# A cross-covariance attention and feed-forward kernel: the sixteen second products of the first token group placed at steps 11 to 31 instead of 11 to 33

## The chip, the cores and the metric

The kernel runs on one core of a Trainium2 chip. The metric is device time in microseconds (us). Beside it each run gives the span, from the first to the last instruction of the core; the time is some 1.7 to 3.0 us longer than the span. All runs here were classed as fast by the clock and the 1.5% limit, with a granted TensorE clock of 0.999 to 1.000. Engines are called by the profile's names: PE (matmuls), PEld (weight loads), ACT (ScalarE), DVE (VectorE), POOL (GpSimd), SP.

## The reference, cut to what matters

```python
def _attn_ref(q, k, v, tau):               # q, k, v: 4 x 6080 x 256
    qn = q / (np.linalg.norm(q, axis=1, keepdims=True) + 1e-06)
    kn = k / (np.linalg.norm(k, axis=1, keepdims=True) + 1e-06)
    s = kn.transpose(0, 2, 1) @ qn / tau
    a = softmax(s)                          # cut: written out in full
    return v @ a
def _moe_ref(x, w_in, w_out, s, b):         # x: 24320 x 256, d_ff = 2048
    r = np.maximum(x @ w_in, 0.0)
    return (s * (r * r) + b) @ w_out
```

## The kernel before

The attention matrix is folded into the weights of the first product: per batch, `wa` is the softmax times `w_in`. The 24,320 tokens are then taken in 48 groups (47 of 512 and a last one of 256), and each group in 16 steps. A step makes one h tile of 128 of the 2,048 features (two 512-column matmuls); after every second step ACT takes the pair of h tiles out of PSUM as `r = relu(h)`. DVE or ACT squares r to `g`. The second product g x w_out comes later, interleaved with the next group's steps. Groups 1 to 46 use seven instead of eight block products ("seven items" per step), which need sums S of g made on DVE. Groups 0 and 47 are "plain": sixteen second products, one per 128 features, each of four 256-column matmuls (two in group 47).

```python
# pools: h_ps 2 buffers (pairs of h tiles), sq_pool 2, o_ps 3
PLAG = {0: 11, NG - 1: 5}
CO = (7, 14, 18, 24)                  # steps of the four casts of w_out; cast 0 on DVE, 1 to 3 on ACT
RC = (13, 16, 19, 21, 23)             # sums for rowconst on DVE; its matmul is at step 30
# ... cut ...
def norm_step(gr=gr, c=c, sc=sc):     # squares and folds of the next batch's q and k, chunk c
    ops = gr.norm_ops(c)              # ACT square, DVE square, DVE fold, DVE fold, ...
    for i, f in enumerate(ops):
        at_step(int(sc) + 2 + 1 + i * 3, f)
# ... cut ...
for s in range(NS + FT):              # FT = 16 steps per group
    g, m = divmod(s, FT)
    if g < NG:
        mm1(g, m)                     # h of this step
    # ... cut: seven items of the group before ...
    for gp in plain:
        for mp in range(FT):
            if s == gp * FT + PLAG[gp] + (mp * 3 // 2 if gp == 0 else mp):
                plain_mm2(gp, mp)     # after the last one: two o_sb evacuations on DVE
    if g < NG and m % 2 == 1:
        relu(g, m // 2)               # ACT
    # ... cut: squares, sums S, then the side work (casts, norms, gram products) of step s ...
```

The kernel holds each engine's instructions to program order (`tc.keep_in_program_order`), and the traces follow it: putting two evacuations back in the program moved them from 64.79 to 67.70 us on DVE (e1 below). So the position of a product in this loop sets what stands behind it.

Of the kernel before, what the change touches and what calls it, by code (L numbers as in the profile page):

```python
# [16 lines left out]
def kernel(  # L17
# [28 lines left out]
    FT = Dff // P  # L46
# [541 lines left out]
    def mm1(g, m):  # L588

        _, nj = group(g)  # L590
        n = nj * P
        vT = vT_tiles[g]
        i, fh = divmod(m, 2)
        if fh == 0:
            h_tiles[g, i] = h_tile("h_ps")
        h_ps = h_tiles[g, i][:, fh, :]
        for b, p0, p1 in segments(g):
            wa = grams[b].wa
            for ci in range(CH):
                if p1 - p0 == P:  # L600
                    dst, src = h_ps[:, :n], vT[:, ci, :n]
                else:
                    dst = h_ps[:, :n].rearrange("f (j p) -> f j p", p=P)[:, :, p0:p1]
                    src = vT[:, ci, :n].rearrange("f (j p) -> f j p", p=P)[:, :, p0:p1]
                po(nc.tensor.matmul(dst, wa[:, ci, ts(m, P)], src,  # L605
                                    start=(ci == 0), stop=(ci == CH - 1), skip_group_check=True))
        if m == FT - 1:
            del vT_tiles[g]

    def relu(g, i):  # L610
        n = group(g)[1] * P
        if i % 2 == 0:
            r_tiles[g, i // 2] = rpool.tile([P, 2, 2, TG], FP16, tag="r16", name="r16")
        r16 = r_tiles[g, i // 2]
        po(nc.scalar.activation(out=r16[:, :, i % 2, :n], in_=h_tiles.pop((g, i))[:, :, :n],  # L615
                                func=AF.Relu))

    def square(g, i0, i1, engine):

        n = group(g)[1] * P  # L620
        if i0 == 0:
            g_tiles[g] = gpool.tile([P, 2, NP, TG], FP16, tag="g16", name="g16")
        src = r_tiles[g, i0 // 2][:, :, i0 % 2 : i0 % 2 + i1 - i0, :n]
        dst = g_tiles[g][:, :, i0:i1, :n]
        if engine is nc.scalar:
            po(nc.scalar.activation(out=dst, in_=src, func=AF.Square))  # L626
        else:
            po(nc.vector.tensor_mul(dst, src, src))  # L628
# [33 lines left out]
    def plain_mm2(g, m):  # L662

        _, nj = group(g)
        if g == NG - 1:
            last_mm2(0, m)
            if m == FT - 1:
                for i in range(FT):
                    last_mm2(1, i)
            return  # L670
        for h in range((nj + 1) // 2):
            js = [j for j in (2 * h, 2 * h + 1) if j < nj]
            if m == 0:
                o_plain[g, h] = ps_o.tile([P, 2, C], FP32, tag="o_ps", name="o_ps")
            o = o_plain[g, h]
            for j in js:
                po(nc.tensor.matmul(  # L677
                    o[:, j % 2, :], g_tiles[g][:, m % 2, m // 2, ts(j, P)],
                    w_out16[:, m, :], start=(m == 0 and j == js[0]),
                    stop=(m == FT - 1 and j == js[-1]), skip_group_check=True))  # L680
            if m == FT - 1:
                if h == 0:
                    o_sbs[g] = opool.tile([P, TG // P, C], FP32, tag="o_sb", name="o_sb")
                evacuate(o_sbs[g][:, js[0] : js[-1] + 1, :], o, rowconst, 1)
                if js[-1] == nj - 1:
                    store(g)
# [4 lines left out]
    def sums_of(g, n, i0=0, i1=NP):  # L691
        G = g_tiles[g][:, :, i0:i1]
        A11, A12 = G[:, 0, :, : TG // 2], G[:, 1, :, : TG // 2]
        A21, A22 = G[:, 0, :, TG // 2 :], G[:, 1, :, TG // 2 :]
        if i0 == 0:
            S[n] = spool.tile([P, NP, TG // 2], FP16, tag=f"S{n}", name=f"S{n}")
        T = {k: t[:, i0:i1] for k, t in S.items()}
        if n == 1:
            po(nc.vector.tensor_add(T[1], A21, A22))  # L699
        elif n == 2:  # L700
            po(nc.vector.tensor_sub(T[2], T[1], A11))  # L701
        elif n == 3:
            po(nc.vector.tensor_sub(T[3], A11, A21))  # L703
        else:
            po(nc.vector.tensor_sub(T[4], A12, T[2]))  # L705
# [77 lines left out]
    PLAG = {0: 11, NG - 1: 5}  # L783
# [13 lines left out]
    for s in range(NS + FT):  # L797
        g, m = divmod(s, FT)
        if g < NG:
            mm1(g, m)  # L800

        if m == SHIFT and 0 < g and g - 1 not in plain:
            items = seven_items(g - 1)
            work.append((items, 8 if g == NG - 1 else 7))
        if work:
            items, n = work[0]
            for f in items[:n]:
                f()
            del items[:n]
            if not items:  # L810
                work.pop(0)
        for gp in plain:
            for mp in range(FT):
                if s == gp * FT + PLAG[gp] + (mp * 3 // 2 if gp == 0 else mp):
                    plain_mm2(gp, mp)
        if g < NG and m % 2 == 1:
            relu(g, m // 2)
            if g in plain:
                late = g > 0 and m // 2 % 2 == 0
                square(g, m // 2, m // 2 + 1, nc.scalar if late else nc.vector)  # L820
        if g < NG and g not in plain and m in SQUARES:
            square(g, *SQUARES[m])
        if g == NG - 1 and m in LAST:
            LAST[m]()
        elif m == 0 and 0 < g and g - 1 not in plain:
            square(g - 1, 6, 8, nc.vector)
        elif 0 < g and g - 1 not in plain and m in SUMS:
            sums_of(g - 1, SUMS[m])
        for f in side.pop(s, []):
            f()  # L830
# [34 lines left out]
```

## Time and profile before

| | before |
|---|---|
| time, median of 3 (lowest to highest) | 720.33 us (720.29 to 720.56) |
| span of the profiled run | 718.5 us |
| busy PE / DVE / ACT / POOL | 97% / 87% / 76% / 15% |
| PE waits listed after the start-up | 0.4, 0.3 and 0.2 us |

Busy shares are averages over the whole span. PE is busy 49.99 or 50.00 us in every 50 from 100 to 700, so what can be won lies in the stretches where PE is not first. The chain that ended last shows these. Line L605 is h, L677 a plain second product, L773 a block product, L615 relu, L504 a cast of w_out, L633 an evacuation of o_ps (to `o_sb` or `u`), L699 to L705 the sums S, L162, L165 and L178 the norm operations. For PE a record's length runs past the start of the next matmul (57.13 + 0.59 against 57.56), so holes are counted from start to start. The lines themselves stand in the prediction.

### The profile page before, as it was taken

The numbers are of one execution on the slowest core, as the hardware profiler recorded it, in microseconds if no ns is written. First come the engines' busy times: TensorE is split into PE (matmuls) and PEld (weight loads), VectorE is DVE, ScalarE is ACT, GpSimd is POOL, SyncE is SP. The second block draws the span as 40 slices with busy tenths as digits, with TensorE's granted clock in tenths as the row PEclk, the third lists the DMA queues.
The fourth block names the chain that finished last, engine by engine and source line by source line (L and its number), as shares of the span: only waits on it lengthen the run. The fifth ranks groups of instructions, "written<-read, shape, count | busy, mean of one in ns | idle before, by whom it ended". The sixth has DMA issues, their size and how long they took to land.

```text
span 718.5 us, 17642 instructions
## 1 busy us (share of the span) xinstructions
PE 699.4 (97%) x7481; PEld 505.0 (70%) x7481; DVE 625.9 (87%) x879; ACT 544.5 (76%) x588; POOL 109.8 (15%) x189
## 2 busy tenths in 40 slices
PE   4799999999999999999999999999999999999998
PEld 3556777776677777777677777777668777777777
DVE  4779999998889999999888899999887888888886
ACT  4489877887777777788777777778877777777875
POOL 4532332201201222111110222110000000000000
PEclk9999999999999999999999999999999999999999
DMA  9999999547565979443973777844423333321202
GB/s 237 207 259 148 172 166 149 110 103 134 103 105 120 153 133 144 105 96 75 152 155 63 139 136 125 154 93 83 105 65 75 92 71 74 97 59 46 83 30 75
DMA packets 89791, 84.27 MB, mean 117 GB/s; under 512 B 59664, under 2 KB 64848, under 8 KB 89712
## 3 DMA queue, kind: packets, MB, share of 16 engines
q0 software_dynamic: 26064, 43.40, 37.7%
q1 hardware_dynamic: 63072, 38.43, 21.5%
q8 instruction: 59, 0.97, 0.5%
q10 hardware_dynamic: 576, 1.31, 0.5%
q14 instruction: 20, 0.16, 0.1%
HBM read 78.91 MB, written 24.90 MB: 144 GB/s over the span
## 4 chain that ended last, share of the span: by engine, by line
PE 92%; DMA 4%; ACT 1%; DVE 1%; POOL 0%; issue 0%; ACTq 0%; POOLq 0%
PE h_ps L605 45%; PE o_ps L773 40%; PE s_ps L142 4%; PE wa_ps L309 2%; DMA qk<-in_q_dram 2%; DMA qk<-in_k_dram 1%; DMA w_in<-in_moe_w_in_dram 1%; ACT r L615 1%; PE o_ps L651 0%; POOL qk L126 0%; PE o_ps L677 0%; ACT g L626 0%; PE idle_ps L442 0%; DVE o_sb L633 0%; DVE sq L162 0%
## 5 line engine op out<-in xcount | busy, mean ns | idle before, releaser
L615 ACT ACTIVATE r<-h_ps 128x1024 f16<-128x1024 f32 (+1 forms) x384 | 387.6, 1013 | 146.9 <-PE h_ps L605 145.0
L605 PE MATMUL h_ps<-vT,wa 128*128 128x512 f16 (+7 forms) x1632 | 451.9, 364 | 0.6 <-ACT r L615 0.4
L773 PEld LDWEIGHTS <-S 128*128 128x128 f16 x2944 | 197.9, 98 | 85.1 <-DVE S L699 0.4
L773 PEld LDWEIGHTS <-g 128*128 128x128 f16 x2208 | 155.0, 98 | 74.1
L628 DVE TENSOR_TENSOR g<-r 128x2048 f16<-128x2048 f16 (+2 forms) x150 | 174.7, 1165 | 15.1 <-ACT r L615 14.9
L773 PE MATMUL o_ps<-T,S 128*128 128x128 f16 x2208 | 183.2, 219 | 0.3 <-DVE S L699 0.2
L605 PEld LDWEIGHTS <-wa 128*128 128x128 f16 x1632 | 136.0, 98 | 21.4 <-issue 1.0
L773 PE MATMUL o_ps<-w_out,g 128*128 128x128 f16 x1472 | 134.2, 219 | 0.3 <-DVE u L633 0.3
L633 DVE SCALAR_TENSOR_TENSOR o_sb<-o_ps,s_out,u 128x256 f32<-128x256 f32 x138 | 66.4, 481 | 47.6 <-PE o_ps L773 45.1
L626 ACT ACTIVATE g<-r 128x1024 f16<-128x1024 f16 (+1 forms) x97 | 100.4, 1035 | 0.2
L142 PE MATMUL s_ps<-qk 128*128 128x256 f16 (+1 forms) x384 | 70.0, 283 | 14.0 <-ACT qk L133 8.7
L361 POOL DMA_DIRECT2D v<-in_v_dram x48 | 31.3, 656 | 263.0 <-DMA vT<-v 199.5
L633 DVE SCALAR_TENSOR_TENSOR u<-o_ps,s_out,rowconst 128x256 f32<-128x256 f32 x138 | 65.9, 478 | 0.0
L773 PE MATMUL o_ps<-w_out,S 128*128 128x128 f16 x736 | 63.4, 219 | 0.0
L773 PE MATMUL o_ps<-N,g 128*128 128x128 f16 x736 | 63.4, 219 | 0.0
L188 POOL DMA_DIRECT2D f<-f x30 | 26.3, 877 | 225.8 <-DVE f L178 167.0
L165 ACT ACTIVATE sq<-qk 128x1024 f16<-128x1024 f16 (+3 forms) x49 | 50.4, 1033 | 10.3 <-DMA qk<-in_k_dram 6.3
L701 DVE TENSOR_TENSOR S<-S,g 128x2048 f16<-128x2048 f16 (+1 forms) x47 | 56.4, 1201 | 1.3
L699 DVE TENSOR_TENSOR S<-g 128x2048 f16<-128x2048 f16 (+1 forms) x47 | 56.0, 1192 | 0.0
L705 DVE TENSOR_TENSOR S<-g,S 128x2048 f16<-128x2048 f16 x46 | 55.9, 1216 | 0.0
L703 DVE TENSOR_TENSOR S<-g 128x2048 f16<-128x2048 f16 x46 | 55.9, 1215 | 0.0
L142 PEld LDWEIGHTS <-qk 128*128 128x128 f16 (+1 forms) x384 | 32.9, 101 | 19.8 <-DVE qk L132 8.1
(75 smaller groups left out, 324.3 us busy)
## 6 DMA issues: line engine op xcount, KB each, us to landing
out_dram<-o_sb SPq DMA_DIRECT2D x46, 512.0 KB, 3.0
v<-in_v_dram POOLq DMA_DIRECT2D x47, 256.0 KB, 4.7
qk<-in_k_dram POOLq DMA_DIRECT2D x42, 256.0 KB, 6.0
qk<-in_q_dram POOLq DMA_DIRECT2D x42, 256.0 KB, 7.2
f<-f POOLq DMA_DIRECT2D x30, 128.0 KB, 3.0
vT<-v SPq DMA_TRANSPOSE x182, 3.2
w<-in_moe_w_out_dram POOLq DMA_DIRECT2D x4, 512.0 KB, 11.4
raw<-in_q_dram ACTq DMA_DIRECT2D x2, 512.0 KB, 6.6
```

Of the source, the lines that this page charges most:

```text
L142: po(nc.tensor.matmul(self.s_ps[:, ch, :], kc[:np_, j, ts(ch, P)], qc[:np_, j, :], start=(c == 0 and j == 0 and ch == 0), stop=(c == len(s ...
L165: po(nc.scalar.activation(out=st["sq"][:np_, 1, js, :], in_=kc[:np_, js, :], func=AF.Square))
L605: po(nc.tensor.matmul(dst, wa[:, ci, ts(m, P)], src, start=(ci == 0), stop=(ci == CH - 1), skip_group_check=True))
L615: po(nc.scalar.activation(out=r16[:, :, i % 2, :n], in_=h_tiles.pop((g, i))[:, :, :n], func=AF.Relu))
L626: po(nc.scalar.activation(out=dst, in_=src, func=AF.Square))
L628: po(nc.vector.tensor_mul(dst, src, src))
L633: po(nc.vector.scalar_tensor_tensor(out=dst, in0=src, scalar=s_out, op0=ALU.mult, in1=add, op1=ALU.add))
L699: po(nc.vector.tensor_add(T[1], A21, A22))
L701: po(nc.vector.tensor_sub(T[2], T[1], A11))
L703: po(nc.vector.tensor_sub(T[3], A11, A21))
L705: po(nc.vector.tensor_sub(T[4], A12, T[2]))
L773: po(nc.tensor.matmul(st[name][:, j, :], a()[:, i, ts(j, P)], w[:, i, :], start=first, stop=last, skip_group_check=True))
```

## The change

It spreads the sixteen plain products of group 0 over steps 11 to 31 instead of 11 to 33. The intent is to place each product, and with it each need for a cast of w_out, where the activations leave PE idle.

```diff
-                if s == gp * FT + PLAG[gp] + (mp * 3 // 2 if gp == 0 else mp):
+                if s == gp * FT + PLAG[gp] + (mp * 4 // 3 if gp == 0 else mp):
```

## The prediction

> **What bounds the kernel now.** I read the page first: its engine shares, its slices, then the chain that ended last. All times are microseconds (us) from the span's start unless another unit is given.
>
> ```profile
> PE 699.4 (97%) x7481; PEld 505.0 (70%) x7481; DVE 625.9 (87%) x879; ACT 544.5 (76%) x588; POOL 109.8 (15%) x189
> PE   4799999999999999999999999999999999999998
> PE 92%; DMA 4%; ACT 1%; DVE 1%; POOL 0%; issue 0%; ACTq 0%; POOLq 0%
> ```
>
> TensorE (PE) ends the kernel: 92% of the chain is its own work. Only 1% is ScalarE (ACT) and 1% VectorE (DVE); that is where a reordering that removes no work could gain anything. The next question is where those stretches lie. The chain in order of time, limited to 49 to 80, answers (start, length, engine and line):
>
> ```profile
> 49.57 1.02 ACT r L615
> 50.59 0.30 ACT w_out L504
> ...
> 55.22 0.94 ACT g L626
> 56.17 0.91 ACT r L615
> 57.08 0.94 ACT g L626
> 58.02 0.92 ACT r L615
> 58.95 0.04 issue
> 58.99 0.59 PE h_ps L605 x2
> ...
> 67.49 1.32 DVE o_sb L633 x2
> 68.82 1.14 DVE S L699
> 69.98 1.23 DVE S L701
> ...
> 74.27 0.41 DVE u L633
> 74.68 0.04 issue
> 74.72 0.22 PE o_ps L773
> ```
>
> The set-up of groups 0 and 1 has two places where PE is not first: from 49.6 to 59.0 ACT carries the chain (activations, casts of w_out, squares), and from 64.6 to 74.7 mostly DVE (evacuation of the first group's output, then the sums S of the second). After 74.7 it is PE again. The PE timeline shows what both cost:
>
> ```profile
> 57.13 0.59 PE L605 MATMUL h_ps<-vT,wa 128*128 128x512 f16 x2
> 57.56 0.60 PE L677 MATMUL o_ps<-w_out,g 128*128 128x256 f16 x4
> 58.00 0.59 PE L605 MATMUL h_ps<-vT,wa 128*128 128x512 f16 x2
> 58.99 0.59 PE L605 MATMUL h_ps<-vT,wa 128*128 128x512 f16 x2 [0.40 <-ACT r L615]
> 70.00 0.45 PE L773 MATMUL o_ps<-T,S 128*128 128x128 f16 x5 [0.20 <-DVE S L699]
> 74.72 0.22 PE L773 MATMUL o_ps<-w_out,g 128*128 128x128 f16 x1 [0.33 <-DVE u L633]
> ```
>
> An "h" pair of matmuls occupies 0.43 between starts (57.13 to 57.56), a "second product" of four small ones 0.44 (57.56 to 58.00). The modelled ends overlap the next start, so I count starts. The h pair at 58.00 should be followed at 58.43; it is followed at 58.99, so the true hole is 0.56, not the listed 0.40. In the same way: 0.09 before 52.50 and 0.29 before 57.13. First-stretch holes: 0.09 + 0.29 + 0.56 = 0.94. In the second: 0.37 before 70.00 (previous two matmuls began at 69.53 and needed about 0.10), a smaller one inside the products near 72.2, and 0.33 before 74.72: some 0.9 together. That 1.8 of 718.5 is all there is to win here.
>
> **What the Trainium skill says.** "TensorE: Matmul & The Clock Gate", section "Wait — 56ns, not 53.3ns?", gives 215.7 ns between starts of warm 512-column matmuls; the trace agrees (0.43 for two). So a PE that is fed has no slack. "ScalarE: Activation LUTs", section "What ACT_TABLE_LOAD costs", has activations with immediate operands at 186 + 0.833 N ns and about 93 ns of overlap between neighbours; for N = 1024 that is 1.04 each, 0.95 start to start. The trace shows 1.02 to 1.08 and 0.91 to 0.94, so ten ACT operations back to back need about 9.3, whatever PE does. "Perfetto Trace Analysis", section "Identifying the Most-Contended Engine", warns that matmul busy share misjudges the distance to a roofline; the trace agrees, since slices marked 9 hide the 0.29 hole before 57.13.
>
> **The change part by part.** Nothing is added or removed: the comparison of instruction orders has equal row counts on every engine. The sixteen second products of group 0 move from steps 11,12,14,15,17,18,20,21,23,24,26,27,29,30,32,33 to 11,12,13,15,16,17,19,20,21,23,24,25,27,28,29,31. ACT keeps its order of operations; on DVE the two o_sb evacuations step ahead of one square (g) and one sq. So the gain is PE work put into holes. I replay the order with the before trace's spacings (h pair 0.43, product 0.44, gram pair 0.22, ACT about 0.93 start to start, 0.05 from ACT end to PE start, 0.03 from PE end to ACT).
>
> 1. *The first cast.* Product 4 now stands at step 16, before h of step 17. It starts at 51.53 by PE's own pace, and the cast of its weights ends at 50.49 + 1.04 = 51.53, plus 0.05: a wait of 0.05.
> 2. *ACT slips.* The h pair of step 17 starts at 52.02 where it started at 51.53, and so its activation at about 52.65 instead of 52.33. From there ACT is saturated through step 26: the whole ACT chain is 0.32 late.
> 3. *PE is fuller.* h of step 26 waits for the activation of step 23, at 58.99 + 0.32 = 59.31. But PE by then has done 12 products instead of 10: 2 x 0.44 = 0.87 more work. Net lead 0.87 - 0.32 = 0.55. The holes on the way become 0.05 (first cast), 0.23 (step 24), 0.13 (step 26), later 0.09 (step 28): 0.50 in place of 0.94, a gain of 0.44 to 0.47. The other casts end 0.2 to 0.9 before they are needed.
> 4. *End of group 0.* The last product starts at 64.38 (was 66.15), h of step 35 at 66.76 (was 67.23): lead 0.47.
> 5. *DVE.* Before, it idled 1.00 ahead of the square at 65.67 (waiting for activation r), then did square, sq and both evacuations in a saturated chain. Now the evacuations (1.32) start at about 64.79, inside that idle time; the square starts at 66.11, sq at 67.25, S (L699) at 67.86 instead of 68.73: 0.87 earlier. Its result is ready at 69.11, and PE wants it at 69.63 - 0.47 = 69.16: the hole of 0.37 closes. The following DVE work (S, u, S, f, sq, u) is saturated and moves by the same 0.87; the second u, which released PE at 74.72, releases it at 73.85.
>
> Sum: 0.47 from PE filling its ACT holes plus about 0.4 from DVE's earlier start, not twice 0.87. PE leaves the second stretch 0.87 earlier. From 75 to 700 PE is busy to 0.05 in every 50, on its own chain, so nothing after should swallow the lead: 720.33 - 0.87 = 719.46, rounded to 719.5.
>
> **Rivals.** *A wait in place of the removed one:* the denser order needs the first and third casts sooner. For it: the first cast has no margin in my replay (51.53 against 51.53), and each 0.1 of wait there also delays ACT's saturated chain. If the wait were 0.4, ACT would be 0.7 late and PE would gain only 0.1 by step 26; the time would be about 719.9 to 720.2. Against it: ACT's order is unchanged and the cast's start hangs on the h pair of step 13, which does not move (48.94).
>
> *ACT stays the bound and takes everything:* it must do the same operations. For it: ten back to back from 49.6 on. Against it: in the old order ACT waited for PE after step 29 (idle 0.49, 0.42, 0.42, 0.20), so a fuller PE recovers there. If all of the ACT slip stuck and DVE gained nothing, the lead would be 0.2: 720.1.
>
> *Hidden or given back:* the DVE gain could be lost if an early operation waits for a transfer rather than for DVE's turn. For it: sq and f wait for loaded qk. Against it: those loads start below 50, and no PE wait for DMA is listed after the start. Then only PE's 0.47 stays: 719.9. Or a later wait for a fixed event returns the time: near 720.3.
>
> **Range and chances.** My replay gives 719.46; partial loss gives 719.9; complete loss 720.3. The three runs before spread 0.27. A gain beyond 1.3 would need nearly all of both stretches' holes to go. I take 719.0 to 720.2. A change of 2% is 14.4, eight times all the holes, so within 2% is practically certain: chances 0.005, 0.99 and 0.005.
>
> **What would show it right or wrong.** Step 1: first product after the cast (L677) at 51.5 to 51.7. Step 2: the casts of w_out at 50.5, 53.6 and 59.1. Step 3: holes in PE starts up to step 29 of about 0.5 in all. Step 4: first L773 product at 67.2 rather than 67.67. Step 5: first o_sb evacuation at about 64.8, S of L699 at 67.9, no PE wait for it, and the u wait ending near 73.9. Span near 717.6. The prediction is wrong if PE waits for the cast by over 0.3, if DVE's S has not moved by more than 0.5, or if a lead at 75 has gone by 700.

## The result, and the profile after

| | before | after |
|---|---|---|
| time, median of 6 | 720.35 us (720.24 to 720.56) | 719.70 us (719.40 to 720.23) |
| span of the profiled run | 718.5 us | 717.6 us |
| spans of the runs after | | 717.5 to 717.9 us |

The ratio is 0.9991, with a 95% interval of 0.9978 to 1.0004. A ratio is computed as the mean time of one kernel's runs over that of the other's of the same rounds, so it is not quite the ratio of the two medians. The interval includes 1: the times alone do not prove a gain. The traces do better: the one kernel that was traced twice (after, and again as e12) took the same PE path to 0.01 us.

The chain of waits after, in order of time, limited to 49 to 80 (start, length, engine and line):

```profile
52.61 1.02 ACT r L615
53.63 0.32 ACT w_out L504
...
56.43 0.92 ACT r L615
57.35 0.04 issue
57.40 0.59 PE h_ps L605 x2
...
64.53 0.23 PE o_ps L677 x2
64.76 0.04 issue
64.79 1.41 DVE o_sb L633 x2
66.20 1.13 DVE g L628
67.33 0.60 DVE sq L162
67.93 1.15 DVE S L699
69.08 0.02 issue
69.11 1.23 DVE S L701
...
73.80 0.04 issue
73.84 0.22 PE o_ps L773
```

ACT carries the chain only up to 57.35 now (before: 58.95). DVE's part starts with the evacuations at 64.79, where before they stood at 67.49 behind the square of group 1. It ends, and PE takes over, at 73.84 instead of 74.72. The timeline of PE after:

```profile
51.54 0.60 PE L677 MATMUL o_ps<-w_out,g 128*128 128x256 f16 x4
57.40 0.59 PE L605 MATMUL h_ps<-vT,wa 128*128 128x512 f16 x2
59.26 0.59 PE L605 MATMUL h_ps<-vT,wa 128*128 128x512 f16 x2
67.18 0.55 PE L773 MATMUL o_ps<-w_out,g 128*128 128x128 f16 x7
69.16 0.44 PE L773 MATMUL o_ps<-T,S 128*128 128x128 f16 x5
73.84 0.22 PE L773 MATMUL o_ps<-w_out,g 128*128 128x128 f16 x1 [0.21 <-DVE u L633]
```

The first S product, at 69.16, follows without a hole (70.00 before). Two later holes stay, counted start to start: 0.25 before 71.55 and 0.49 before 73.84. From 73.84 on PE keeps its lead: the last run of 21 matmuls starts at 711.97, and at 712.80 before. The lead is 0.88 at 73.84 and 0.83 at the end; 0.04 of each was there before the first changed instruction (transposes at 48.45 and 48.49).

### The profile page after: what moved, and what is told of

It is laid out like the page before. It is cut to its first block, busy times and chain, and to the rows that moved or that the text cites. A ratio compares the mean times of both kernels' runs of the same rounds, so it can differ in the third digit from the quotient of the medians. Undisturbed runs are those within 1.5% of the kernel's fastest.

```text
span 717.6 us, 17642 instructions
## 1 busy us (share of the span) xinstructions
PE 699.5 (97%) x7481; PEld 505.1 (70%) x7481; DVE 626.0 (87%) x879; ACT 544.4 (76%) x588; POOL 110.1 (15%) x189
## 4 chain that ended last, share of the span: by engine, by line
PE 93%; DMA 4%; DVE 1%; ACT 1%; POOL 0%; issue 0%; ACTq 0%; POOLq 0%
PE h_ps L605 45%; PE o_ps L773 40%; PE s_ps L142 4%; PE wa_ps L309 2%; DMA qk<-in_q_dram 2%; DMA qk<-in_k_dram 1%; DMA w_in<-in_moe_w_in_dram 1%; PE o_ps L677 1%; PE o_ps L651 0%; ACT r L615 0%; POOL qk L126 0%; PE idle_ps L442 0%; DVE o_sb L633 0%; DVE S L701 0%; DVE sq L162 0%
## 5 line engine op out<-in xcount | busy, mean ns | idle before, releaser
L773 PEld LDWEIGHTS <-S 128*128 128x128 f16 x2944 | 198.0, 98 | 84.8 <-issue 0.4
L773 PEld LDWEIGHTS <-g 128*128 128x128 f16 x2208 | 155.1, 98 | 74.1
L773 PE MATMUL o_ps<-T,S 128*128 128x128 f16 x2208 | 183.3, 219 | 0.1
L773 PE MATMUL o_ps<-w_out,g 128*128 128x128 f16 x1472 | 134.2, 219 | 0.2 <-DVE u L633 0.2
L773 PE MATMUL o_ps<-w_out,S 128*128 128x128 f16 x736 | 63.4, 219 | 0.0
L773 PE MATMUL o_ps<-N,g 128*128 128x128 f16 x736 | 63.4, 219 | 0.0
L699 DVE TENSOR_TENSOR S<-g 128x2048 f16<-128x2048 f16 (+1 forms) x47 | 56.1, 1193 | 0.0
```

The lines of the kernel that those rows point to most:

```text
L699: po(nc.vector.tensor_add(T[1], A21, A22))
L773: po(nc.tensor.matmul(st[name][:, j, :], a()[:, i, ts(j, P)], w[:, i, :], start=first, stop=last, skip_group_check=True))
```

## The experiments

**Theory:** two chains meet in the second stretch. PE must get there, and DVE must get through evacuation, square, S, and two u. PE leaves when the later of the two is done. The change moves both: PE by filling its holes behind ACT, DVE because the evacuations now stand before the square, in idle time. **Main rival:** the gain is PE's filled holes alone, each worth its own length. **Second rival:** the gain is DVE's alone.

To compare runs whose starts differ by up to 0.4 us, I take times from one point ahead of the change, T, the start of the transposes of group 1. P is the first block product (L773), Y the first product of the fourth block product, where PE waited for the second u; E is the start of the last run of matmuls. These are from the PE timelines; V, the start of group 0's evacuations, is from the DVE timelines.

| kernel | T | P | V | Y | E | E - T | against before | median span |
|---|---|---|---|---|---|---|---|---|
| before | 48.49 | 67.67 | 67.41 | 74.72 | 712.80 | 664.31 | | 718.5 to 718.6 |
| after | 48.45 | 67.18 | 64.79 | 73.84 | 711.97 | 663.52 | -0.79 | 717.8 |
| e1 evacuation held | 48.79 | 67.52 | 67.70 | 75.01 | 713.08 | 664.29 | -0.02 | 718.6 |
| e2 last two early | 48.52 | 67.70 | 65.30 | 74.35 | 712.49 | 663.97 | -0.34 | 718.4 |
| e3 front only | 48.55 | 67.28 | 67.37 | 74.67 | 712.75 | 664.20 | -0.11 | 718.4 |
| e4 casts early | 48.50 | 66.73 | 64.60 | 73.65 | 711.74 | 663.24 | -1.07 | 717.4 |
| e6 after, norms later | 48.82 | 67.55 | 65.16 | 73.47 | 711.92 | 663.10 | -1.21 | 717.2 |
| e9 before, norms later | 48.63 | 67.81 | 66.96 | 73.74 | 712.19 | 663.56 | -0.75 | 717.9 |
| e7 cast late | 48.56 | 68.58 | 66.19 | 75.24 | 713.43 | 664.87 | +0.56 | 719.1 |
| e5 casts early, norms later | 48.47 | 66.70 | 64.57 | 72.63 | 711.08 | 662.61 | -1.70 | 716.8 |

Median spans are of 5 runs (after and e13: 6; before: 9 or 10). The runs of e1 to e4 shared one chip and one set of runs before; e5, e6, e7 and e9 shared another of each; e10 to e12 shared a third set of runs before, and e13 had that set and one run more. Outputs were correct in all.

The table holds a regularity that sharpens the theory. In the seven kernels with the norms in their old place (before, after, e1 to e4, e7) Y comes 9.05 after V where the evacuations stand ahead of the square, and 7.30 or 7.31 after V where they stand behind it. So DVE's chain sets Y in all seven, and PE's filled holes count there only as far as they let the evacuations start earlier. Ahead of the square these start 0.42 or 0.43 after the start of the last plain product (after, e2, e7), unless rowconst holds them (e4).

### e1: the change with the evacuations put back behind the square

```diff
-                evacuate(o_sbs[g][:, js[0] : js[-1] + 1, :], o, rowconst, 1)
+                held.append(...)      # the same call, run at step 33
```

> The changed kernel with PE's order kept, but group 0's two o_sb evacuations put back behind the square g and sq on VectorE, as in the kernel before. Theory (the vector chain from evacuation to the sums S to the second u sets when PE leaves the stretch; a PE lead alone is only waited away): first L773 product still at 67.2 us, S of L699 at about 68.7 (not 67.9), a PE hole of about 0.8 us before the first S product at 70.0, u wait ending at 74.7; span 718.4 +- 0.2, no gain over the kernel before. Rival (filling PE's holes is worth its own 0.47 us whatever VectorE does): span 718.0.

PE's order is that of the change. P - T is 18.73, exactly as after (18.73; before 19.18). But DVE is back in its old order, and its timeline and PE's read:

```profile
67.70 1.40 DVE L633 SCALAR_TENSOR_TENSOR o_sb<-o_ps,s_out,rowconst 128x512 f32<-128x512 f32 x2
69.02 1.21 DVE L699 TENSOR_TENSOR S<-g 128x2048 f16<-128x2048 f16 x1
70.29 0.45 PE L773 MATMUL o_ps<-T,S 128*128 128x128 f16 x5 [0.64 <-DVE S L699]
```

PE's lead of 0.45 is waited away in one hole (0.80 start to start, 0.37 before), and E - T is that of the kernel before to 0.02. Main rival refuted: it wanted 0.47. The span of the profiled run, 720.0, missed the expected 718.4, while the other four were 718.3 to 718.6. The excess lies after the work: the last DVE evacuation started at 715.58 (before: 715.30), yet the span ended at 720.0 (before: 718.5); what follows that evacuation is the last store. The ratio of times is 0.9999 (0.9987 to 1.0012).

### e2: the kernel before with only the last two products moved, to steps 30 and 31

```diff
-  (mp * 3 // 2 if gp == 0 else mp)
+  (mp * 3 // 2 - 2 * (mp >= 14) if gp == 0 else mp)
```

> The kernel before with only the last two second products of group 0 moved, from steps 32 and 33 to 30 and 31. PE's holes behind the activations stay (0.94 us in all up to step 29), so PE has no lead at step 35 (first L773 product at 67.6 to 67.7). Theory (vector chain): the evacuations enter VectorE's idle time at about 65.3, S of L699 starts at 68.3 to 68.4, the hole before 70.0 closes, and PE leaves at about 74.35: a gain of 0.35 to 0.45, span 718.1. Rival (only the filling of the holes behind the activations counts): span 718.5.

```profile
65.30 1.41 DVE L633 SCALAR_TENSOR_TENSOR o_sb<-o_ps,s_out,rowconst 128x512 f32<-128x512 f32 x2 [0.17 <-PE o_ps L677]
```

P - T is 19.18, as before: PE gained nothing. The evacuations started at 65.30, as soon as PE's last plain product released them, and S at 68.36, and Y came 0.40 earlier from T than before. E - T fell by 0.34. DVE's half of the change alone gives somewhat less than half of the gain. The profiled span was 718.1, the expected value; the median of five 718.4 and the ratio 0.9994 (0.9982 to 1.0007) cannot tell it from before.

### e3: the change without its last two products

```diff
-  (mp * 4 // 3 if gp == 0 else mp)
+  ((mp * 3 // 2 if mp >= 14 else mp * 4 // 3) if gp == 0 else mp)
```

> The changed kernel with only its last two second products put back to steps 32 and 33; the other fourteen as in the change. Theory (vector chain): PE reaches step 35 with a lead of about 0.45 us (first L773 product at 67.2), but the evacuations start at about 67.4 and S of L699 at 68.7 as in the kernel before; the lead is waited away before the first S product; span 718.4 +- 0.2. Rival (PE's filled holes are worth 0.47 by themselves): span 718.0.

P - T is 18.73: fourteen products suffice for PE's whole lead. S of L699 started at 68.69, and E - T gained 0.11, within what was expected for the span (718.4). With e1 this is the second way to give PE its lead and DVE nothing, and it again yields next to nothing. The halves measured alone, 0.11 and 0.34, add up to 0.45, while both together gave 0.79: they cannot be added. DVE's half keeps its gain alone; PE's half needs it, and on top of it brings 0.45 (0.79 less 0.34).

### e7: the change with cast 1 one step later

```diff
-    CO = (7, 14, 18, 24)
+    CO = (7, 15, 18, 24)
```

> The changed kernel with the cast 1 of w_out at step 15 (behind the activation of steps 14 and 15) instead of step 14. Theory (the product at step 16 has no margin for that cast): the cast runs at about 51.75 to 52.8, product 4 starts at 52.85 instead of 51.54, a PE hole of 1.3 us, and the activations behind it slip by up to as much; some 0.9 to 1.3 us lost against the changed kernel by the first L773 product (68.1 to 68.5), span 718.5 to 719.0, so at or above the kernel before. Rival (ScalarE's total of work is what matters, not the place of a cast): span stays 717.6.

```profile
51.17 0.59 PE L605 MATMUL h_ps<-vT,wa 128*128 128x512 f16 x2
52.94 0.60 PE L677 MATMUL o_ps<-w_out,g 128*128 128x256 f16 x4 [1.18 <-ACT w_out L504]
```

The product should have followed the h pair at 51.60; it started at 52.94, a hole of 1.34. P, V and Y are each 1.29 later from T than after, E - T is 1.35 longer, and the median span of 719.1 is above that of the kernel before. P (68.58) and the span lie just above the expected ranges. The change has indeed no margin at its first cast, and a hole here passes through whole: DVE's evacuations are as late as PE.

### e4: the change with casts 1 and 2 two steps earlier

```diff
-    CO = (7, 14, 18, 24)
+    CO = (7, 12, 16, 24)
```

> The changed kernel with the casts 1 and 2 of w_out moved from steps 14 and 18 to 12 and 16, where ScalarE waits for PE (1.20 and 0.19 us idle), so that they leave its saturated stretch. Both theories: the PE holes before the h pairs of steps 24 and 26 (0.22 and 0.13 us) close, first L773 product at about 66.75 instead of 67.18. Theory (vector chain): the evacuations cannot start before rowconst is done on VectorE (64.65), so S moves by at most 0.2 us; span 717.4. Rival (PE's lead counts in full): span 717.15.

The casts now run where ACT waited for PE. P comes 18.23 after T, 0.50 earlier than after; the holes up to step 26 are gone. But rowconst holds DVE until 64.5, the evacuations started at 64.60 instead of 64.79, and E - T gained only 0.28 over after. So the theory's cap is seen again, near its predicted 0.2. The ratio to before is 0.9975 (0.9962 to 0.9989), the first that excludes 1. It flatters the kernel a little: the nine runs before in this set had a median of 720.89, and 720.35 beside the changed kernel.

### e6 and e9: norm operations of the next batch put off, in the kernel after and the one before

```diff
-                    at_step(int(sc) + 2 + 1 + i * 3, f)
+                    at_step(int(sc) + 2 + 1 + i * 3 + (max(0, 12 - c) if gr.b == 1 else 0), f)
```

> The changed kernel with the norm operations (squares and folds on ScalarE and VectorE) of the second batch's first chunks put off by 12 steps for chunk 0, 11 for chunk 1 and so on, so that none stands on VectorE between the evacuation of group 0 and the second u. Theory (this vector chain holds PE at 71.55 and 73.84): S of L699 starts at 67.25 instead of 67.85, the PE holes of about 0.25 and 0.5 us close, the first Y product starts at about 73.1; span 716.9, if the put-off work costs nothing later. Rival (those holes are PE's own pace or activations): no move, span 717.6.

> The kernel before with the same put-off of the norm operations. Theory (PE's lead of 0.47 and VectorE's lead of 0.87 are not a sum: PE leaves at the later of the two): with VectorE out of the way the evacuations start at 66.8, S at 68.15, all three later PE holes (0.37, 0.25, 0.5) close, span about 717.4; and the difference to the changed kernel with the same put-off shrinks from 0.9 to PE's own 0.45 to 0.55 us. Rival (the gain of the change comes from VectorE alone): with norms put off both kernels have the same span to 0.15.

With squares and folds out of DVE's chain, PE has no hole left between P and Y in either kernel. In e6 the end reads so (six such matmuls take 0.33 from start to start):

```profile
73.14 0.50 PE L773 MATMUL o_ps<-T,S 128*128 128x128 f16 x6
73.47 0.22 PE L773 MATMUL o_ps<-w_out,g 128*128 128x128 f16 x1
```

S of L699 came 0.49 earlier from T than after, where 0.60 was expected. In the kernel before Y falls 1.12 earlier from T, in the kernel after 0.74 earlier. E - T differs between the two by 0.46, and P - T by 0.45: PE's filled holes count in full exactly where DVE no longer sets the end. The second rival, which wanted equal spans, is refuted (medians 717.9 and 717.2).

Both kernels gave 0.32 to 0.37 back: E - Y is 638.07 to 638.19 in all kernels of the table with the norms in their old place, and 638.45 in e5, e6 and e9. Comparing the starts of the same activations after and in e6, the lead shrinks near 100 and near 135 us. So the expected spans were missed, for e6 by 0.3 (median 717.2 for 716.9) and for e9 by 0.5 (717.9 for 717.4).

### e5: casts early and norms later together

The edits are those of e4 and e6, both in the changed kernel.

> The changed kernel with both the casts 1 and 2 at steps 12 and 16 and the norm operations put off. Theory: with VectorE out of the way PE's extra lead of 0.45 from the earlier casts counts in full, where it counted 0.2 to 0.25 with the norms in their old place; the first Y product starts at about 72.65; span 716.4. Rival (rowconst on VectorE caps the start of the evacuations at 64.6 and so everything after): span 716.7, 0.2 below the put-off alone.

Y fell at 72.63 as expected, and the extra PE lead of the early casts counted 0.49 (662.61 against 663.10 in e6), where with the norms in place it had counted 0.28. The span, 716.7 to 716.9 in four of five runs and 718.4 in one, missed 716.4 by the 0.37 that the put-off gives back; the expectation had left that out. It lies near the rival's 716.7, but not for the rival's reason: that wanted a gain of 0.2 over e6, and it was 0.49 in E - T. The ratio to before is 0.9977 (0.9964 to 0.9989). By its trace this is the fastest kernel, 1.70 ahead of before; by times it cannot be told from e4.

### e10, e11, e12, e13: shorter put-offs, and why they fail

```diff
-  (max(0, 12 - c) if gr.b == 1 else 0)          # e5
+  (max(0, 8 - 3 * c) if gr.b == 1 else 0)       # e10
+  (max(0, 12 - 4 * c) if gr.b == 1 else 0)      # e11; e12 is the changed kernel once more
```

> Casts 1 and 2 early, and the norm operations put off by 8 steps for chunk 0, 5 for chunk 1, 2 for chunk 2 and none after. Theory (the put-off of all chunks by up to 12 steps gave back 0.37 us because squares and folds then met later sums on VectorE near 100 and 135 us): the holes of the second stretch stay closed (first Y product near 72.65), the lead is no longer given back, span 716.3 to 716.5. Rival (VectorE must do this work before 150 anyway, and whatever leaves the stretch returns as a hole): span 716.7 to 716.8 as with the long put-off.

> The same with 12, 8, 4 steps and none after. Theory: as the short put-off, span 716.3 to 716.5. Rival: 716.7 to 716.8.

> The changed kernel again, in the same rounds as its two descendants: span 717.5 to 717.9, first L773 product 18.73 us after the first transpose of group 1 (19.18 in the kernel before). Theory and rival agree; it is the yardstick for the other two.

e10, e11 and e13 keep the early casts of e5. Theory and rival were both wrong for e10 and e11: median spans 718.3 and 719.7, E - T 664.10 and 665.64, so up to 3 us worse than e5. The yardstick e12 repeated the changed kernel to 0.01 in E - T (712.26 - 48.74 = 663.52; median span 717.7, ratio 0.9989, 0.9976 to 1.0001). I had moved each chunk by a different amount and so pushed the first four chunks closer together. In e11 the waits read so, first PE's and then ACT's:

```profile
77.35 0.22 PE L773 MATMUL o_ps<-T,S 128*128 128x128 f16 x1 [0.63 <-ACT T L508]
81.99 0.59 PE L605 MATMUL h_ps<-vT,wa 128*128 128x512 f16 x2 [0.48 <-ACT r L615]
85.99 0.45 PE L773 MATMUL o_ps<-T,S 128*128 128x128 f16 x5 [0.61 <-DVE S L699]
89.39 0.33 PE L773 MATMUL o_ps<-T,S 128*128 128x128 f16 x3 [1.03 <-DVE u L633]
79.97 1.06 ACT L165 ACTIVATE sq<-qk 128x1024 f16<-128x1024 f16 x1 [1.75 <-issue]
83.88 1.06 ACT L165 ACTIVATE sq<-qk 128x1024 f16<-128x1024 f16 x1 [1.03 <-issue]
```

The two stalls of ACT name no releaser, but each ends 0.08 after a fold on DVE ends (79.89 and 83.80), and there are two buffers of squares. Test e13 gives e11 four (of the first folds too, which come from the same pool):

```diff
-    sq_pool = pool("sq_pool", 2)
+    sq_pool = pool("sq_pool", 4)
```

> The 12, 8, 4 put-off with the pool of squares at 4 buffers instead of 2. The medium put-off had cost 3.0 us against the long one; its ScalarE trace has two stalls, 1.75 us before the square at 79.97 and 1.03 before that at 83.88, each ending 0.08 us after a fold on VectorE (79.89, 83.80), with activations queued behind. Theory (the two buffers of squares are held by unfinished folds, and ScalarE, in order, makes PE wait): both stalls go, and with them the PE holes at 81.99 (0.54) and, as they come from late activations, most of that at 85.99 (0.61); those at 77.35 (cast of T behind a square, 0.63) and 89.39 (second u behind squares and folds, 1.0) stay; span about 718.6. Rival (crowding of VectorE and ScalarE alone): span 719.5 to 719.8.

```profile
PE o_ps L773 <- DVE u L633: 1.0, 1, 1.0
PE o_ps L773 <- ACT T L508: 0.6, 1, 0.6
```

In the list of PE's waits (waiter, line, releaser: total, times, longest) after the start-up only these two are left of the four. The squares start at 78.09 and 81.87 without a stall, and the profiled span is 718.6 as expected (median 718.8, e11 719.7). From T to E, e11 took 665.64 and e13 664.45 (712.92 - 48.47): the two-buffer pool cost 1.2 of the 3.0 that e11 lost against e5. The rest stands in the waits for a cast of T and for u; that the order of squares and folds made those late is read from the trace, not tested. For e10 the cause was read from its trace alone, in part: it too waits for a cast of T and for u. What e5 gives back near 100 and 135 us was not tested further.

## Why the prediction was right

It said 719.5 with 719.0 to 720.2; the median is 719.70.

- **Step 1, the first cast:** the product was to start between 51.5 and 51.7; it started at 51.54. The lack of margin is shown by e7.
- **Step 2, ACT's slip of 0.32:** casts were to start at 50.5, 53.6 and 59.1; they started at 50.45, 53.53 and 59.08.
- **Step 3, remaining PE holes of 0.50:** counted start to start they are 0.04, 0.22, 0.13 and 0.13, in all 0.52.
- **Step 4, P at 67.2:** 67.18.
- **Step 5, evacuation at 64.8, S at 67.9, no wait for S, u's wait ending at 73.9:** 64.79, 67.85, none, 73.84. Span "near 717.6": 717.6.
- **The sum:** the total of 0.87 was right to 0.08, counted from T. Its two summands, "0.47 from PE filling its ACT holes plus about 0.4 from DVE's earlier start", hold in one order only. The new place of the evacuations alone (e2) brings Y 0.40 forward, and PE's filled holes on top of it 0.44 more, because the last product, and with it V, comes that much earlier. PE's filled holes alone are worth 0.02 to 0.11 (e1, e3), so the third rival's "then only PE's 0.47 stays: 719.9" names a value that should have been close to 720.3. e6 and e9 show the opposite case, in which PE sets Y and its 0.46 counts by itself.
- **A mis-sized term:** "some 0.9 together" for the second stretch mixes true holes with the listed 0.33. Start to start the three are 0.37, 0.26 and 0.50, in all 1.13, and e9, which closes all three, brings Y 1.12 forward. So some 2.1 was to win in the two stretches, not 1.8. Only the prediction's bounds rest on this sum, not its forecast.
- **What the number alone shows:** little. The range 719.0 to 720.2 also holds the 719.9 and 720.1 that the prediction gave to its rivals; the steps above and e1 to e3 decide between them.
- **The time:** the medians differ by 0.65, the spans of the profiled runs by 0.9. The time outside the span varied from 1.7 to 3.0 us, and some runs had a span 0.9 to 1.6 us above the median of their kernel. An effect of 0.8 us is therefore seen in E - T, and only just not in the interval of the times.

## What to carry to other kernels

Where two engines' chains meet, moving work of one forward gains only up to the other's arrival; work out both arrival times from the trace before adding gains together. A lead can also count through the other engine: here PE's filled holes paid because the evacuations waited for PE's last product. A program-order position changes more than the engine it is written for: here the last product's place moved two evacuations into another engine's idle time, and that decided whether the first engine's lead was kept. When putting work off, keep the spacing: pushing chunks together filled a pool of two buffers and stalled ACT, with its activations queued behind, for 1.75 us.

## What the Trainium skill lacked or had wrong

- "ScalarE: Activation LUTs", section "What ACT_TABLE_LOAD costs": the 1.04 us for 1,024 elements and 0.95 from start to start in the prediction are estimates from its formula. They fit to some hundredths: relu from PSUM took 1.01 to 1.05 (median 1.02), squares from SBUF 1.04 to 1.09 (median 1.05), and starts lay 0.91 to 0.94 apart.
- No page that I read gives the hand-over between engines in numbers. Here PE started about 0.05 us after the end of the ACT operation it waited for (end 57.34, start 57.40), and ACT 0.03 to 0.05 after the end of PE's record, which is modelled (49.54 to 49.57 before, 52.56 to 52.61 after).
- "Perfetto Trace Analysis", section "Optimization Strategy", says that a gap that repeats on the engine that should be saturated can mean too little space for the next tile. It speaks of that engine alone: in e11 gaps with this cause sat on ACT, which was not the saturated engine, and only e13's extra buffers confirmed them (1.75 and 1.03 us, gone with four buffers).
- No page that I read tells how far repeated executions differ at the end of a kernel: in e1's profiled run the span ended 1.5 us later than before though its last evacuation started only 0.28 later, and the time outside the span ran from 1.7 to 3.0 us.
